# Dropping GpSimd's port waits from two feed-forward blocks and keeping them in the attention before them

## The chip, the cores and the metric

The program runs on one core of one Trainium2 chip. The metric is the time of one execution on the device, in microseconds. Four compute engines work at once and each takes its instructions in a fixed order: TensorE (PE; its weight loads are listed as PEld), VectorE (DVE), ScalarE (ACT) and GpSimd (POOL). SyncE (SP) issues the DMAs. Engines wait for one another through semaphores.

## What is computed

A causal attention with a decay (4 batches, 8 heads, 576 positions, head size 64), and behind it two feed-forward blocks on its output (2304 tokens, width 512, inner width 2048), all in float32:

```python
def _attn_ref(q, k, v, f):
    scores = scale * np.matmul(q, k.transpose(0, 1, 3, 2))
    cum = np.cumsum(np.log(np.clip(f, 0.0001, 1.0)), axis=-1)
    decay = cum[:, :, :, None] - cum[:, :, None, :]
    scores = np.where(causal, -1000000000.0, scores + decay)
    ...                                    # softmax over the last axis
    return np.matmul(attn, v)

def _moe_ref(x, w_in, w_out):              # first block
    h = x @ w_in
    g = np.where(h >= 1, h, np.where(h <= -1, 0.0, (h + 1) ** 2 / 4))
    return g @ w_out

def _moe2_ref(x, w_in, w_out, a, b):       # second block
    h = x @ w_in
    P = a[0] + a[1] * h + a[2] * h**2 + a[3] * h**3
    Q = 1.0 + np.abs(b[0]) * np.abs(h) + np.abs(b[1]) * h**2
    return (P / (Q + 1e-06)) @ w_out
```

## The kernel before

To reach float32's accuracy with TensorE's fp32r matmuls, every operand is split in a high and a low part: ScalarE writes the high part (a cast), and VectorE or GpSimd subtract it from the operand for the low one. Each product is then three matmuls: low by high, high by low, high by high. The tiles are named for this: `xh` and `xl` for the input of the first block, `gh` and `gl` for the activated values, `uh` and `ul` and parts of `arena` for the operands of the second block. The weights arrive as 64-bit floats, and VectorE converts them in four steps on tiles `wd` (each step 128 by 512 elements, SBUF to SBUF) behind one step of ScalarE.

The kernel runs in three stages. In the attention (to about 212 us in the trace), the matmuls of the first block's early part fill gaps. From about 212 to 540 us the first block runs in passes over chunks of 512 or 256 tokens; weights of the second block are converted and stored on the side (`t_q`, `wd`). From about 540 us the second block runs: its first product is made of seven smaller ones (L1059, a Winograd scheme of 2 by 2 blocks) on banks `h`, with additions on VectorE (`h<-h,us`), and its second product (L1085) adds into banks `a0` to `a3` (`b` in the trace).

The order of all instructions comes from a planner written out in the kernel. `plan` is a list scheduler: each task has ways (an engine with a duration), and the planner keeps a clock for each engine and picks the task that can start first. It has one more resource, `port`: VectorE tasks of the kind `dvp` (all inputs and the output in SBUF) and GpSimd's tasks share it, one at a time. For each GpSimd task that the plan starts less than `NEAR` = 1.0 us behind the end of the last `dvp` task, it notes that task in `behind` (L371 to L376). `emit` then issues the tasks in the planned order. Where a GpSimd task stands in `behind`, `emit` adds a dependency: the task's first GpSimd instruction waits for the last VectorE instruction of the noted task, though it needs no data of it. `Kept` (L18 to L31) is a wrapper that remembers what was issued on VectorE and GpSimd. The plan itself does not depend on whether that dependency is added.

`emit` is called twice, first for the attention (with `filling` set to `True`), then for the two blocks (`filling` is `False` there). The plan notes 93 GpSimd tasks in the first call and 72 in the second.

All VectorE and GpSimd instructions pass through the wrapper, so the trace shows them with one line, L26; they are told apart by their tiles.

Of the kernel before, what the change touches and what calls it, by code (L numbers as in the profile page):

```python
# [32 lines left out]
def kernel(ctx, tc, qT, kT, v, f, w_in1, w_out1, w_in2, w_out2, a, b, out):  # L33
    nc = tc.nc
    PE, ACT, DVE, POOL, SP = nc.tensor, nc.scalar, Kept(nc.vector), Kept(nc.gpsimd), nc.sync
# [267 lines left out]
    behind, given_to = {}, {}  # L303
# [837 lines left out]
    filling = True  # L1141
# [9 lines left out]
    for size, kind, x, k in pieces:  # L1151
        key = FS + (FE - FS) * sofar / whole
        sofar += size
        n = CH[x]
# [27 lines left out]
    for kk in range(KD):  # L1182
        n = CH[FILL]
# [24 lines left out]
    def emit(order):  # L1208

        for n, fn in order:  # L1210
            DVE.given, POOL.given = [], []
            fn()
            given_to[n] = DVE.given
            if n in behind and POOL.given and given_to[behind[n]]:
                tc.add_manual_dep(POOL.given[0].ins, given_to[behind[n]][-1].ins.name, after_it, reason="port")

    bufs.update({tag: [T0] * n for tag, n in N_BUF.items()})
    nudge(0)
    order_ = plan(0, WK)
    emit(order_)  # L1220
    filling = False
    att.close()
# [88 lines left out]
    for p, (m, x, fs) in enumerate(passes):  # L1311
        n = CH[x % NCH]
# [71 lines left out]
    n = QN  # L1384
# [117 lines left out]
    nudge(first)  # L1502
    order_ = plan(first, WKB)
    emit(order_)
    man.close()

# [45 lines left out]
```

## Time and profile before

| | |
|---|---|
| median of 3 runs | 947.63 us (947.58 to 947.81) |
| the profiled execution | 947.47 us, span 945.8 us |
| TensorE busy | 933.6 us (99% of the span) |
| VectorE busy | 738.6 us (78%) |
| ScalarE busy | 704.7 us (75%) |
| GpSimd busy | 443.2 us (47%) |

The span is the time from the first to the last instruction; the rest of the execution's time lies around it. An engine is busy while it executes an instruction of the program; waiting does not count, but an instruction that is held up after its start does, and appears longer. So the busy share alone doesn't tell a held engine from a working one; the duration of an instruction beside others of its shape does.

### The profile page before, as it was taken

The page shows a single profiled execution, that of the slowest core. Times are in us where ns is not written, and L with a number is a line of the kernel's source. Part 1 is how long each engine was busy: PE and PEld are TensorE (multiplying, and loading weights), DVE is VectorE, ACT ScalarE, POOL GpSimd, SP SyncE. Part 2 cuts the span into 40 slices and gives each one's busy share as a digit, 9 for nine tenths or more (in the row PEclk, how much of TensorE's full clock was granted, in tenths as well). Part 3 has the DMA queues.
Part 4 walks back from the last instruction along what each step waited for, and adds up shares of the span by engine and source line. Part 5 has one row for each costly group of instructions (what it writes and reads, how often), then busy time and mean ns, then how long its engine had stood idle before and what let it go on. Part 6 is the DMA issues. An engine that isn't in the chain of part 4 may idle for free.

```text
span 945.8 us, 16658 instructions
## 1 busy us (share of the span) xinstructions
PE 933.6 (99%) x5172; PEld 789.3 (83%) x5172; DVE 738.6 (78%) x1615; ACT 704.7 (75%) x1568; POOL 443.2 (47%) x542
## 2 busy tenths in 40 slices
PE   9899999999999999999999999999999999999998
PEld 6666877778888888888998888989898989898986
DVE  8989789873766987887557598899988888888840
ACT  7899888875765655655556599889988898878751
POOL 3655633636465222131222176666655556555553
PEclk9999999999999999999999999999999999999999
DMA  8788898846554477686947856877334473434100
GB/s 256 231 276 268 249 304 269 272 158 202 178 178 161 163 261 262 199 283 229 326 138 258 283 196 189 265 225 255 141 138 145 140 241 114 141 132 150 34 34 34
DMA packets 107489, 188.55 MB, mean 199 GB/s; under 512 B 13108, under 2 KB 43460, under 8 KB 107400
## 3 DMA queue, kind: packets, MB, share of 16 engines
q1 hardware_dynamic: 107400, 187.48, 59.9%
q8 instruction: 41, 0.67, 0.3%
q14 instruction: 48, 0.39, 0.1%
HBM read 142.72 MB, written 44.71 MB: 198 GB/s over the span
## 4 chain that ended last, share of the span: by engine, by line
PE 87%; DMA 5%; DVE 4%; ACT 2%; issue 1%; SPq 1%; POOL 0%; DVEq 0%; POOLq 0%; ACTq 0%
PE b L1085 21%; PE h L799 20%; PE h L1059 19%; PE a L901 18%; PE T L573 3%; PE O L610 2%; PE a L890 2%; DMA cb<-cd 2%; PE S L507 1%; DVE P L26 1%; DMA raw<-in_moe_w_in_dram 1%; PE S L498 1%; DVE wd L26 1%; DMA rcd<-rr 1%; ACT P L561 1%
## 5 line engine op out<-in xcount | busy, mean ns | idle before, releaser
L26 POOL TENSOR_TENSOR gl<-t,gh 128x512 fp32r<-128x512 f32 (+2 forms) x125 | 139.9, 1126 | 218.1 <-ACT gh L815 87.1
L1085 PE MATMUL b<-w,gh 128*128 128x512 f32 x576 | 179.1, 392 | 0.0
L901 PE MATMUL a<-gh,w 128*128 128x512 f32 (+1 forms) x576 | 161.8, 366 | 0.0
L26 POOL TENSOR_TENSOR t<-t,t 128x384 f32<-128x384 f32 x96 | 97.6, 1019 | 97.0 <-ACT t L847 77.9
L1085 PEld LDWEIGHTS b<-w,gh 128*128 128x128 f32 x576 | 108.0, 188 | 21.1
L26 DVE SCALAR_TENSOR_TENSOR t<-h,t 128x512 f32<-128x512 f32 (+2 forms) x125 | 73.7, 601 | 60.5 <-ACT t L831 59.7
L799 PE MATMUL h<-xh,arena 128*128 128x512 f32 (+1 forms) x400 | 120.1, 368 | 0.1
L901 PEld LDWEIGHTS a<-gh,w 128*128 128x128 f32 x576 | 104.0, 189 | 17.2
L1085 PE MATMUL b<-w,gl 128*128 128x512 f32 x288 | 112.0, 389 | 0.0
L815 ACT CAST gh<-t 128x512 fp32r<-128x512 f32 (+2 forms) x125 | 68.7, 553 | 49.4 <-PE a L901 25.5
L901 PE MATMUL a<-gl,w 128*128 128x512 f32 (+1 forms) x288 | 105.3, 366 | 0.0
L26 DVE SCALAR_TENSOR_TENSOR wd<-raw,wd 128x512 int32<-128x512 int32 x128 | 96.9, 758 | 2.6
L1059 PE MATMUL h<-arena,q 128*128 128x384 f32 x459 | 93.2, 336 | 0.0
L561 ACT ACTIVATE P<-P,nm 128x576 f32<-128x576 f32 (+2 forms) x144 | 83.7, 583 | 12.6 <-DVE nm L26 12.1
L826 ACT ACTIVATE t<-h 128x512 f32<-128x512 f32 (+1 forms) x77 | 42.5, 552 | 60.2 <-PE h L799 56.8
L26 DVE TENSOR_SCALAR wd<-wd 128x512 f32<-128x512 f32 (+1 forms) x128 | 67.1, 525 | 23.9 <-ACT wd L109 22.3
L1059 PEld LDWEIGHTS h<-arena,q 128*128 128x128 f32 x459 | 81.3, 188 | 4.5 <-DVE h L26 1.2
L799 PEld LDWEIGHTS h<-xh,arena 128*128 128x128 f32 x400 | 73.0, 188 | 12.9 <-DVE t L26 0.5
L799 PE MATMUL h<-xl,arena 128*128 128x512 f32 (+1 forms) x200 | 73.6, 368 | 0.0
L26 POOL TENSOR_SCALAR_AFFINE_SELECT cb<-cb 128x128 f32<-128x128 f32 (+1 forms) x150 | 43.8, 305 | 58.5 <-DVE wd L26 26.3
L26 DVE CUSTOM_DVE_ANT_0 P<-S,cb 128x256 f32<-128x256 f32 (+1 forms) x135 | 62.5, 477 | 10.6 <-POOL cb L26 4.3
L573 PE MATMUL T<-ident,P 128*128 128x128 f32 x400 | 63.5, 280 | 6.3 <-DVE PT L26 4.0
(171 smaller groups left out, 2214.5 us busy)
## 6 DMA issues: line engine op xcount, KB each, us to landing
q<-wqd SPq DMA_DIRECT2D x46, 512.0 KB, 3.7
raw<-in_moe_w_in_dram SPq DMA_DIRECT2D x32, 512.0 KB, 5.3
raw<-in_moe_w_out_dram SPq DMA_DIRECT2D x32, 512.0 KB, 4.1
arena<-wqd SPq DMA_DIRECT2D x26, 512.0 KB, 3.6
cb<-cd SPq DMA_DIRECT2D x15, 576.0 KB
xr<-xd SPq DMA_DIRECT2D x32, 256.0 KB, 3.3
wqd<-t SPq DMA_DIRECT2D x32, 256.0 KB, 3.8
wfd<-wd SPq DMA_DIRECT2D x26, 256.0 KB
```

What stands on the lines that cost most here:

```text
L26: self.given.append(getattr(self.engine, name)(*args, **kwargs))
L498: PE.matmul(t[:, 0:n1 - n0], lhs, rhs, start=(x == 0), stop=(x == len(ways) - 1))
L561: ACT.activation(p, p, AF.Exp, scale=-1.0, bias=nm[pr][:, pos:pos + 1], accum_out=ls[pr][:, COL[pos]:COL[pos] + 1])
L573: PE.transpose(ps[:, (c - c0) * P:(c - c0 + 1) * P], p[:, k0:k0 + P], ident[:])
L610: PE.matmul(o[pp, c_q:n], nat[pr, 2][:, c, pp], pt[:, c, j, c_q:n], start=(c == 0), stop=(c == ncs - 1),)
L799: PE.matmul(hps[g], ww[:, kk * P:(kk + 1) * P], xx[kk], start=(kk == 0 and y == 0), stop=(kk == KD - 1 and y == 2))
L815: ACT.copy(gt[g][0], mid[g][0][:, 0:n])
L826: ACT.activation(s[:, 0:n], hps[g], AF.Relu, scale=0.5, bias=0.5)
L890: PE.matmul(acc[x, d], ww[:, dd], gg, start=(part == 0 and g == gs[0]), stop=(part == 2 and g == gs[-1]))
L901: PE.matmul(acc[x, d], ww[:, dd], gg, start=(first and y == 0), stop=(last and y == 2))
L1059: PE.matmul(o, ww, xx, start=(new and i == 0 and z == 0), stop=(i == HQ - 1 and z == 2), skip_group_check=True,)
L1085: PE.matmul(acc[x, d], gg[:, dd], ww, start=(g == 0 and y == 0), stop=(g == NF - 1 and y == 2))
```

## The change

One condition more in `emit`: the dependency is added only while `filling` is true, which is the attention. In the two blocks a GpSimd instruction no longer waits for the VectorE operation noted in `behind`. The plan, the order of each engine's instructions and all other dependencies stay.

```diff
@@ -1211,7 +1211,7 @@
             DVE.given, POOL.given = [], []
             fn()
             given_to[n] = DVE.given
-            if n in behind and POOL.given and given_to[behind[n]]:
+            if filling and n in behind and POOL.given and given_to[behind[n]]:
                 tc.add_manual_dep(POOL.given[0].ins, given_to[behind[n]][-1].ins.name, after_it, reason="port")
```

## Rows read from the trace of the kernel before

**Rows 1.** Busy time by stretch: PE, PEld, DVE, ACT, POOL (instructions), clock, DMA.

```profile
540.00:640.00 100.00, 100.00 (x501) 89.56 (x500) 91.29 (x178) 88.17 (x184) 63.14 (x58) 1.00 0.68 219
```

**Rows 2.** Waits of PEld, 212 to 946 us: total us, times, longest; first and last.

```profile
PEld h L1059 <- DVE h L26: 1.2, 3, 0.4
...
PEld h L1059 <- DVE tailh L26: 0.3, 1, 0.3
```

**Rows 3.** Timeline at 229 us: start, us, engine, operation, [idle before <-releaser].

```profile
229.26 1.29 POOL L26 TENSOR_TENSOR arena<-wf,arena 128x512 fp32r<-128x512 f32 x1
229.35 1.75 DVE L26 TENSOR_TENSOR xl<-xr,xh 128x512 fp32r<-128x512 f32 x1 [0.34 <-ACT xh L783]
```

**Rows 4.** Timeline at 87 us, and the mask's group on the page (busy, mean ns).

```profile
86.83 1.36 DVE L26 SCALAR_TENSOR_TENSOR wd<-raw,wd 128x512 int32<-128x512 int32 x2
87.53 0.81 POOL L26 TENSOR_SCALAR_AFFINE_SELECT cb<-cb 128x128 f32<-128x128 f32 x1 [1.72 <-DVE wd L26]
88.11 0.84 DVE L26 TENSOR_TENSOR kl<-ks,kh 128x576 fp32r<-128x576 f32 x1
...
L26 POOL TENSOR_SCALAR_AFFINE_SELECT cb<-cb 128x128 f32<-128x128 f32 (+1 forms) x150 | 43.8, 305 | 58.5 <-DVE wd L26 26.3
```

**Rows 5.** Timeline 513 to 518 us, and the wd group on the page.

```profile
513.18 1.30 POOL L26 TENSOR_TENSOR gl<-t,gh 128x512 fp32r<-128x512 f32 x1 [3.82 <-DVE t L26]
513.78 1.45 DVE L26 TENSOR_SCALAR wd<-wd 128x512 f32<-128x512 f32 x2 [0.74 <-ACT wd L109]
514.65 0.61 ACT L815 CAST gh<-t 128x512 fp32r<-128x512 f32 x1
515.26 1.42 DVE L26 SCALAR_TENSOR_TENSOR wd<-raw,wd 128x512 int32<-128x512 int32 x2
516.85 1.30 POOL L26 TENSOR_TENSOR gl<-t,gh 128x512 fp32r<-128x512 f32 x1 [2.37 <-DVE wd L26]
517.33 0.19 PEld L799 LDWEIGHTS h<-xh,arena 128*128 128x128 f32 x1 [0.53 <-DVE t L26]
...
L26 DVE TENSOR_SCALAR wd<-wd 128x512 f32<-128x512 f32 (+1 forms) x128 | 67.1, 525 | 23.9 <-ACT wd L109 22.3
```

**Rows 6.** Timeline 541 to 549 us.

```profile
541.87 0.62 ACT L815 CAST gh<-t 128x512 fp32r<-128x512 f32 x1 [0.58 <-PE a L901]
...
544.64 0.56 DVE L26 COPY us<-h 128x384 f32<-128x384 f32 x1 [0.47 <-PE h L1059]
545.09 0.58 ACT L847 ACTIVATE t<-h,rt 128x384 f32<-128x384 f32 x1
...
545.58 1.02 DVE L26 TENSOR_TENSOR ul<-ul,uh 128x384 fp32r<-128x384 f32 x2
...
547.46 0.55 DVE L26 COPY us<-h 128x384 f32<-128x384 f32 x1
547.62 1.02 POOL L26 TENSOR_TENSOR t<-t,t 128x384 f32<-128x384 f32 x1 [2.58 <-DVE arena L26]
...
548.62 1.22 PE L1059 MATMUL h<-arena,q 128*128 128x384 f32 x6
```

**Rows 7.** Timeline 627 to 634 us.

```profile
627.55 0.58 ACT L847 ACTIVATE t<-h,rt 128x384 f32<-128x384 f32 x1
627.97 1.14 DVE L26 TENSOR_TENSOR xq<-xq,xq 128x384 f32<-128x384 f32 x2
...
629.25 1.01 POOL L26 TENSOR_TENSOR t<-t,t 128x384 f32<-128x384 f32 x1 [1.16 <-ACT tailh L850]
...
629.99 0.58 ACT L847 ACTIVATE t<-h,rt 128x384 f32<-128x384 f32 x1
630.02 0.67 DVE L26 TENSOR_TENSOR xq<-xq,xq 128x384 f32<-128x384 f32 x1
...
632.07 1.01 DVE L26 SCALAR_TENSOR_TENSOR t<-h,t 128x384 f32<-128x384 f32 x2
633.00 1.23 PE L1059 MATMUL h<-arena,q 128*128 128x384 f32 x6
```

## The prediction

> **What bounds the kernel now.** I read first the busy table by stretch, then TensorE's own waits, then GpSimd's, then the timeline around single waits. In the two blocks TensorE is the bound: from 540 to 640 us it is busy 100.00 of 100.00 us, beside VectorE at 91.29 and GpSimd at 63.14 [rows 1]. Its ends are modelled, so the better measure is what its weight loads wait for from 212 us on: four kinds of wait, the largest 1.2 us for VectorE's h, the smallest 0.3 us for VectorE's tailh, 2.3 us in all and none for GpSimd [rows 2]. So the most that this stretch can give back is about 2.3 us (0.24%), and no GpSimd wait is on that list. What can be lost has no such bound: TensorE takes its work in a fixed order, and each time that VectorE is later than a matmul's start, the delay goes to the end.
>
> **What the waits do.** The plan marks GpSimd operations that should start behind a VectorE operation which uses SBUF alone; in the blocks it marks 72 of them, in the attention 93. The 72 go, the 93 stay. No instruction, transfer or order on a queue is added, moved or removed; GpSimd's true waits (for ScalarE's data, for free buffers) stay. A GpSimd operation may therefore start as soon as its data and GpSimd itself are there.
>
> **The port, as the rows show it.** VectorE operations with both inputs in SBUF and GpSimd operations exclude one another, in both directions. GpSimd's split at 229.26 runs to 230.55; VectorE's xl, begun at 229.35, takes 1.75 us and ends 0.55 after GpSimd [rows 3]. The other way, GpSimd's mask at 87.53 takes 0.81 us where its group takes 0.305: it got the port about 0.14 us before VectorE's wd ended at 88.19. VectorE's next one, kl, began at 88.11, before wd had ended, and still came second: it ends at 88.95, 0.61 after GpSimd [rows 4]. So a GpSimd operation that becomes ready in the middle of a VectorE chain gets in at the next joint, and the rest of the chain is late by most of its 1.0 to 1.3 us. With the wait it goes behind the chain, where VectorE mostly has operations on PSUM that don't care: us at 547.46 takes 0.55 us although GpSimd runs from 547.62 [rows 6].
>
> The Trainium skill's page "SBUF — State Buffer", section "Who interferes with whom", says the same of the port: issue order decides who blocks, for the whole instruction. That speaks against this change, and the trace agrees (1.75 us for xl). The same page gives the loser's start as VectorE's end plus about 0.115 us (in its section on the wrong bandwidth-pool intuition). By that figure a chain whose next operation begins before the last has ended would keep the port, and the places below would cost nothing; the 88.11 row says otherwise, since kl began first and lost.
>
> **Where nothing changes.** If the awaited VectorE operation is already running when GpSimd is ready, the port holds GpSimd as the semaphore did. The gain is then 0.1 to 0.3 us of GpSimd time, which no TensorE wait asks for: 0. In the first block most chains are conversions of weights, needed several us later; the earlier GpSimd operation costs VectorE about 1 us there, hidden by VectorE's idle share (8.7 of 100 us even in the densest stretch [rows 1]; more before 540): 0, unless the chain ends in something that TensorE takes within 1 us. That is so in three places that I priced, in profile time.
>
> A, end of the first block, 513 to 517 [rows 5]. GpSimd's split at 513.18 had been idle 3.82 us, and would run in that idle time; the wd pair at 513.78 took 1.45 us, against 1.05 by its group's mean of 0.525, and would then end some 0.4 earlier. But the next split has its data at 515.26 (ScalarE's gh, 514.65 + 0.61). It gets in between the two wd of the pair that began at 515.26, now 0.4 earlier; the second ends about 0.55 after GpSimd (515.4 + 1.30 + 0.55 = 517.25 against 516.68). What follows there is the t that TensorE already waits 0.53 us for at 517.33. Cost 0.55; without the 0.4 in advance 0.95.
>
> B, start of the second block, 541 to 549 [rows 6]. VectorE splits the new operands just ahead of TensorE. Two GpSimd operations now get in: gl (its data stands at 541.87 + 0.62 = 542.49, in the middle of the chain), and t (data at 545.09 + 0.58 = 545.67 instead of 547.62). The first delays the chain by about 1.1, of which the 0.47 idle before us at 544.64 takes part, so 0.55 is passed on; the second lets VectorE's second ul of the pair at 545.58 go on only at about 547.1, which brings the lag to 1.4. The us that ends at 548.01 ends at 549.4; TensorE took it at 548.62, so with 0.06 us to start, 0.8 is lost. If the first is absorbed wholly, the lag is 0.83 and the loss 0.3. I take 0.8.
>
> C, 628 to 633 [rows 7]. The first t on GpSimd has its data at 628.13 (627.55 + 0.58) against a start at 629.25. It gets in between the two xq that begin at 627.97, and the second ends at 629.8 for 629.11: 0.7 late. The next t has data at 630.57, ready at about 630.65, and the next xq would now begin at 630.72 (630.02 + 0.7): whoever wins, VectorE is 0.7 or 1.4 late. The first of the two t at 632.07 ends at 632.61; TensorE starts on its bank at 633.00. Loss 0.35 or 1.05; I take 0.6, nearer the lower since 0.07 us decides.
>
> **Other early starts.** Of the rest, a few lie before work that TensorE takes within 1 us (splits of the next chunk's x, a copy of an output bank, a bank that VectorE frees). No row prices these as a whole. Bounds: 0, if all are hidden as in the first block, and 2.0, the price of B two and a half times. I take 0.5, nearer to 0 since most of the awaited operations are conversions. Below nothing is excluded for these, as TensorE waits for no GpSimd operation [rows 2], but B and C can be given back in part: at most the 2.3 us.
>
> **Sum.** 0.55 + 0.8 + 0.6 + 0.5 = 2.45 us on the profiled execution's 947.47 (span 945.8 and 1.67 around it): 949.92. The median of the runs stands 0.16 above that execution, so 950.1 us, +0.26%.
>
> **Rivals.**
> 1. The port does the waits' work: GpSimd is held at the port where it was held by the semaphore, or TensorE's lead is enough after all. Then only A, or less, is left: 947.6 to 949.4, no change that can be told. For it: the 2.3 us show that TensorE rides with little loss though VectorE is often stretched already (1.75 at 229.35 [rows 3]); against it: B and C, where the lead is 0.6 and 0.4.
> 2. Faster: GpSimd's results come up to 2 us earlier, ScalarE's logarithm behind t starts earlier, and the banks come free sooner. It decides where ScalarE waits for GpSimd, not for itself. At most the 2.3 us of [rows 2] would go: 945.3. Against it: those waits name VectorE, which gets later, not sooner. To be faster by over 1.9 us it would need nearly all.
> 3. Pile-up: VectorE has 8.7 us of idle in 100 [rows 1]; if each of some eight early starts there costs it 1.0, the idle is gone and VectorE is the bound from 540 to 640. Then A to C come in full (0.95 + 0.8 + 1.05) and the others at 2.0: +4.8, 952.4.
> 4. That the change does nothing at all is excluded: the marked waits are seen in the trace as GpSimd idle behind VectorE, 3.82 us before 513.18 [rows 5].
>
> **Chances.** A measurement here tells about 0.2% (1.9 us) from no change. Forecast (+1.9 to +3.6) 0.45; rival 1 0.42; rival 2 0.03; rival 3 0.10. So faster 0.03, same 0.42, slower 0.55. The range holds the forecast and nearly all of rival 1 and the lower end of rival 3: 947.5 to 952.2. The forecast's own range is 949.5 to 951.2.
>
> **What would show it.** GpSimd's idle time behind VectorE's wd, t and arena goes from the blocks. VectorE's busy time grows by 5 to 20 us, in stretched wd, arena, ul and xq groups, at unchanged counts. TensorE's waits for VectorE grow from 2.3 to about 5 us, at 517, 547 to 549 and 633. If VectorE's mean times don't grow, the port account is wrong; if they grow and TensorE's waits do not, the leads were longer than I read; if the total grows by over 5 us, a queue that I have not seen (the conversions feed stores and loads on SP) has become late.

## The result, and the profile after

| | before | after |
|---|---|---|
| median | 947.72 us (947.58 to 948.11) | 953.12 us (952.91 to 953.4) |
| span of the profiled execution | 945.8 us | 951.4 us |

The ratio is 1.0058, 95% interval [1.0045, 1.007]: 5.4 us slower. The sign was forecast; the size was not (950.1 us, at most 952.2).

The busy line of the page after:

```profile
PE 935.3 (98%) x5172; PEld 788.9 (83%) x5172; DVE 755.3 (79%) x1615; ACT 705.6 (74%) x1568; POOL 452.4 (48%) x542
```

The counts are those of before. VectorE is busy 16.7 us longer (738.6 before), GpSimd 9.2 (443.2 before): the same instructions, held after their start. Busy time by stretch, after, answers [rows 1]; the columns are those of that group:

```profile
540.00:640.00 100.00, 97.04 (x481) 85.85 (x481) 90.18 (x168) 84.46 (x175) 63.36 (x57) 1.00 0.66 215
```

TensorE, at 100.00 of 100.00 before, now loses 3 us between 540 and 640, at an unchanged clock. What its weight loads wait for from 212 us on, after, answers [rows 2] (total us, times, longest):

```profile
PEld h L1059 <- issue: 1.9, 1, 1.9
PEld h L1059 <- DVE h L26: 1.4, 4, 0.4
PEld h L1059 <- DVE t L26: 1.2, 1, 1.2
PEld h L1059 <- ACT arena L1026: 1.0, 1, 1.0
PEld b L1085 <- DVE osb L26: 0.9, 1, 0.9
PEld a L901 <- issue: 0.9, 1, 0.9
PEld a L901 <- DVE t L26: 0.4, 1, 0.4
PEld h L1059 <- ACT us L419: 0.3, 1, 0.3
```

That is 8.0 us for 2.3, 6.7 of it behind VectorE with the two "issue" rows, as these stand behind matmuls that themselves wait for VectorE (its t at 406.66, its h at 554.88).

The list gives waits, not where the time is lost for good. For that I paired TensorE's 5172 matmuls of two runs in order and took, for each, its start after minus its start before. The difference is a stair. Its steps, from the level ahead of a place to the level behind it, are the price of each place (they stand against the start of the matmul in the run before, in us):

| place | step after | priced at |
|---|---|---|
| 405.6, the matmuls of L901 (a), for VectorE's t | +0.71 | 0 ("hidden") |
| 467.9, L901 again | +0.50 | 0, or within the others' 0.5 |
| 517.3 (A) | -0.40 | +0.55 |
| 548.6 (B) | +0.85 | +0.8 |
| 551.1, the next sum of six | +1.78 | not seen |
| 633.0 (C) | +1.05 | +0.6 |
| 666.8, for an output bank | +0.74 | within the others' 0.5 |

Between the steps the stair is flat to 0.1 us, apart from a step back of 0.14 at 619 us and from the start-up: 0.5 us before 25 us here, and -0.1 to 1.0 in the runs below, whatever their edit. The seven steps sum to 5.2, the two medians differ by 5.4. A stair is made of one execution of each kernel; where several kernels below drop the same waits, their steps agree to 0.05 us, except at 468 and 517.

Three places in detail. The timeline after at 388 to 407 us, the place that had been called hidden (start, us, engine, operation; x2 is two in a row; the idle time before, and its releaser, in brackets):

```profile
388.31 1.42 POOL L26 TENSOR_TENSOR gl<-t,gh 128x512 fp32r<-128x512 f32 x1 [1.43 <-ACT gh L815]
388.62 2.39 DVE L26 SCALAR_TENSOR_TENSOR wd<-raw,wd 128x512 int32<-128x512 int32 x2
...
392.25 0.89 DVE L26 TENSOR_SCALAR wd<-wd 128x512 f32<-128x512 f32 x2 [0.65 <-ACT wd L109]
393.18 2.38 DVE L26 SCALAR_TENSOR_TENSOR wd<-raw,wd 128x512 int32<-128x512 int32 x2
393.39 1.62 POOL L26 TENSOR_TENSOR gl<-t,gh 128x512 fp32r<-128x512 f32 x1 [3.66 <-ACT gh L815]
...
401.12 1.85 POOL L26 TENSOR_TENSOR gl<-t,gh 128x512 fp32r<-128x512 f32 x1 [6.11 <-ACT gh L815]
401.13 0.69 DVE L26 SCALAR_TENSOR_TENSOR wd<-raw,wd 128x512 int32<-128x512 int32 x1
401.74 1.52 DVE L26 TENSOR_SCALAR wd<-wd 128x512 int32<-128x512 int32 x1
...
405.83 1.28 DVE L26 TENSOR_TENSOR t<-a,t 128x512 f32<-128x512 f32 x2
...
406.66 0.47 PE L901 MATMUL a<-gl,w 128*128 128x512 f32 x1 [0.46 <-DVE t L26]
```

A pair of wd takes 1.42 us when it runs alone; here 2.39, 2.38, and then a single wd 1.52 instead of 0.43. Three times about 1 us; the idle time before 392.25 takes up little of it, as ScalarE's wd that ends it comes later too. The t that began at 402.66 before begins at 405.83. TensorE had a lead of 2.23 us over it (403.34 to 405.57), which covers two of the three.

The timeline after at 543 to 555 us answers [rows 6]:

```profile
543.90 1.65 POOL L26 TENSOR_TENSOR gl<-t,gh 128x512 fp32r<-128x512 f32 x1 [1.14 <-ACT gh L815]
544.32 1.65 DVE L26 TENSOR_TENSOR arena<-arena 128x384 fp32r<-128x384 f32 x1
...
548.02 1.16 POOL L26 TENSOR_TENSOR t<-t,t 128x384 f32<-128x384 f32 x1 [2.47 <-ACT t L847]
548.37 1.69 DVE L26 TENSOR_TENSOR arena<-arena 128x384 fp32r<-128x384 f32 x2
...
549.98 0.55 DVE L26 COPY us<-h 128x384 f32<-128x384 f32 x1
...
550.67 1.28 PE L1059 MATMUL h<-arena,q 128*128 128x384 f32 x6 [0.63 <-ACT gh L815]
550.80 1.29 POOL L26 TENSOR_TENSOR gl<-t,gh 128x512 fp32r<-128x512 f32 x1 [1.62 <-ACT gh L815]
551.11 2.69 DVE L26 TENSOR_TENSOR arena<-arena 128x384 fp32r<-128x384 f32 x2
552.36 1.02 POOL L26 TENSOR_TENSOR t<-t,t 128x384 f32<-128x384 f32 x1 [0.27 <-ACT t L847]
...
554.19 0.55 DVE L26 TENSOR_TENSOR h<-h,us 128x384 f32<-128x384 f32 x1
...
554.88 1.28 PE L1059 MATMUL h<-arena,q 128*128 128x384 f32 x6 [1.54 <-DVE h L26]
```

GpSimd's idle time now ends with ScalarE's gh and t, not with VectorE's arena. Four GpSimd operations each hold an arena; the prediction followed the first two. The pair at 551.11 takes 2.69 us where two free ones take about 1.0: both are held, one by gl, one by the t behind it. The matmul at 550.67 is the one that stood at 548.62. Its wait is put down to ScalarE's gh, but VectorE's us, whose bank it takes, ends at 550.53, 0.14 us ahead of it, just as VectorE's h ends 0.14 ahead of the next sum (554.74 and 554.88).

C after, which answers [rows 7]:

```profile
630.10 1.02 POOL L26 TENSOR_TENSOR t<-t,t 128x384 f32<-128x384 f32 x1
630.14 1.40 DVE L26 TENSOR_TENSOR xq<-xq,xq 128x384 f32<-128x384 f32 x1
...
632.57 1.41 DVE L26 TENSOR_TENSOR xq<-xq,xq 128x384 f32<-128x384 f32 x2
...
637.70 0.79 PE L1059 MATMUL h<-arena,q 128*128 128x384 f32 x3 [0.79 <-DVE t L26]
```

The first xq is held whole (1.40 for 0.55), and TensorE waits for VectorE's t at the end.

### The profile page after: what moved, and what is told of

Its sections match the earlier page's. It is cut to its first block, busy times and chain, and to the rows that moved or that the text cites. A ratio compares the mean times of both kernels' runs of the same rounds, so it can differ in the third digit from the quotient of the medians.

```text
span 951.4 us, 16638 instructions
## 1 busy us (share of the span) xinstructions
PE 935.3 (98%) x5172; PEld 788.9 (83%) x5172; DVE 755.3 (79%) x1615; ACT 705.6 (74%) x1568; POOL 452.4 (48%) x542
## 4 chain that ended last, share of the span: by engine, by line
PE 85%; DVE 8%; DMA 3%; ACT 2%; issue 2%; POOL 0%; SPq 0%; DVEq 0%; ACTq 0%; POOLq 0%
PE b L1085 20%; PE h L799 19%; PE h L1059 18%; PE a L901 17%; PE T L573 3%; PE O L610 2%; PE S L507 2%; PE a L890 2%; DVE wd L26 2%; DVE P L26 2%; PE warm L692 1%; ACT P L561 1%; PE S L498 1%; DVE PT L26 1%; DVE t L26 1%
## 5 line engine op out<-in xcount | busy, mean ns | idle before, releaser
L26 POOL TENSOR_TENSOR gl<-t,gh 128x512 fp32r<-128x512 f32 (+2 forms) x125 | 146.3, 1177 | 212.9 <-ACT gh L815 168.0
L901 PE MATMUL a<-gh,w 128*128 128x512 f32 (+1 forms) x576 | 161.7, 366 | 0.0
L901 PEld LDWEIGHTS a<-gh,w 128*128 128x128 f32 x576 | 104.0, 189 | 17.1
L26 DVE SCALAR_TENSOR_TENSOR wd<-raw,wd 128x512 int32<-128x512 int32 x128 | 109.1, 854 | 2.6
L901 PE MATMUL a<-gl,w 128*128 128x512 f32 (+1 forms) x288 | 105.4, 366 | 0.7 <-DVE t L26 0.7
L26 DVE TENSOR_SCALAR wd<-wd 128x512 f32<-128x512 f32 (+1 forms) x128 | 64.7, 507 | 21.9 <-ACT wd L109 20.3
```

The costliest lines, as they stand in the source:

```text
L26: self.given.append(getattr(self.engine, name)(*args, **kwargs))
L901: PE.matmul(acc[x, d], ww[:, dd], gg, start=(first and y == 0), stop=(last and y == 2))
```

## Experiments: which waits carry the loss

All but one of them (the limit NEAR, below) edit the one condition in emit. The theory: of the 72 waits taken away, ten stand where a step begins, and only those ten matter; the port holds VectorE at the other places too, but TensorE's lead covers it. The rival: the loss is spread over the 72, as VectorE's grown busy time is.

**Ten waits put back into the changed kernel.**

```
-            if filling and n in behind and POOL.given and given_to[behind[n]]:
+            if n in behind and (filling or n in (2397, 2430, 2593, 2830, 3030, 2843, 3368, 3346, 3357, 3479)) and POOL.given and given_to[behind[n]]:
```

> The changed kernel, with ten of the 72 dropped waits put back: those of the GpSimd operations that got into VectorE's chains just ahead of the five places where TensorE fell behind (tasks 2397 and 2430 before 405 us, 2593 before 468, 2830, 3030 and 2843 at 541 to 551, 3368, 3346 and 3357 at 626 to 631, 3479 at 664). Theory (a few early starts in the wrong joints cost all of it): these ten bring the loss of about 5.2 us back, 947.7 to 948.7 us. What is left open between those ends is the place at 517 us, where no wait is put back: by the predicted price A it costs 0.55. Rival (the loss is spread over the 72, each early start costs VectorE and so TensorE a little): ten of 72 bring back a seventh of it, about 952.4 us.

Measured: 947.46 us, ratio to before 1.0001 [0.9992, 1.001].

```profile
PE 933.1 (99%) x5172; PEld 789.0 (83%) x5172; DVE 745.9 (79%) x1615; ACT 705.7 (75%) x1568; POOL 449.9 (48%) x542
```

VectorE still spends 7.3 us more than before, and nothing is lost. The 62 other waits are worth nothing that the time can tell (it tells about 1 us), and growth of VectorE's busy time is by itself no price. That the time lies under the expected range is due to 517 us: the stair steps back by 0.19 there, where the prediction had a cost of 0.55.

**The same ten dropped from the kernel before.**

```
-            if n in behind and POOL.given and given_to[behind[n]]:
+            if n in behind and n not in (2397, 2430, 2593, 2830, 3030, 2843, 3368, 3346, 3357, 3479) and POOL.given and given_to[behind[n]]:
```

> The kernel before, with only those ten waits dropped and the other 62 of the blocks kept. Theory (ten early starts cost all): 952 to 953.2 us, TensorE's steps at 405, 468, 548, 551, 633 and 667 us as in the changed kernel. Rival (spread over the 72): a seventh of the loss, about 948.5 us. Were both this and the kernel that keeps the ten in the middle, the loss would need both kinds together.

Measured: 953.25 us, 1.0061 [1.0048, 1.0075], the whole loss. The stair has steps at the same places: 0.74, 0.17, -0.40, 0.85, 1.77, 1.05, 0.77. The second, at 468, is 0.3 smaller than in the changed kernel: that part of it needs others of the 62 to be free as well. VectorE is busy 748.1 us: 9.5 us of holding cost 5.5, where the 7.3 of the run before cost 0.

**Every wait dropped, the attention's 93 as well.**

```
-            if n in behind and POOL.given and given_to[behind[n]]:
+            if n in behind and False and POOL.given and given_to[behind[n]]:
```

> All 165 marked waits dropped, those 93 of the attention too. If the joints of VectorE's chains are what the waits guard, the attention, where GpSimd's operations are mostly masks of 0.3 us and VectorE is busy 87 of 100 us, should lose less per wait than the blocks: 953 to 956 us. If a wait is worth the same everywhere (5.4 us for 72), the 93 cost 7 more: 960 us. If the attention's waits cost more than they guard, under 953.

Measured: 957.62 us, 1.0107 [1.0093, 1.0121], between the 953 to 956 and the 960 us of the expectation. So the 93 are worth about 4.5 us more. In the profiled execution (958.31 us) the stair has +1.3 at 44.6 us and some 2.6 more up to 58 us, then +0.97 at 167 us, of which 0.3 is back by 191. Busy time by stretch of this kernel, then of the kernel before:

```profile
46.00:48.00 2.00, 0.66 (x4) 0.47 (x5) 2.00 (x7) 0.85 (x3) 0.56 (x3) 0.86 0.83 269
48.00:50.00 2.00, 2.00 (x15) 1.88 (x16) 1.12 (x6) 2.00 (x6) 1.40 (x6) 0.50 0.97 370
```

```profile
48.00:50.00 2.00, 2.00 (x17) 1.32 (x16) 2.00 (x10) 2.00 (x8) 1.22 (x4) 1.00 1.00 388
```

TensorE is busy only 0.66 of the 2 us to 48, its longest wait there 1.23 us for VectorE's nm. Then the granted clock stands at 0.50 of full speed (1.2 GHz) from 48 to 50, where before it was 1.00. A matmul of 256 columns takes 0.52 us at 48.42, where two of 384 in a row took 0.34 at 43.58.

This fall is not the main part of what the 93 waits are worth. The last kernel below keeps all 93, and its profiled execution has the like: TensorE busy 0.87 of the 2 us from 38 to 40, and then (busy time by stretch)

```profile
42.00:44.00 2.00, 2.00 (x10) 0.99 (x9) 1.93 (x6) 1.17 (x3) 1.58 (x2) 0.50 0.75 280
```

And of the four executions with every wait dropped, the one with a mean granted clock of 1.0 took 956.94 us, 3.8 more than the changed kernel's median; the two at 0.996 took 958.31 and 958.87. So most of the 4.5 us comes without the fall. Where it comes from stays open, as the one trace of this kernel has the fall in it.

## Experiments: place A

**One wait dropped from the kernel before, that of the split at 513.18.**

```
-            if n in behind and POOL.given and given_to[behind[n]]:
+            if n in behind and n != 2778 and POOL.given and given_to[behind[n]]:
```

> The kernel before, with one wait dropped: that of the split that ran at 513.18 us after 3.82 us of idle (task 2778). Theory (a GpSimd operation that runs in an idle stretch of VectorE takes nothing, and frees the port for later): the wd at 513.78 is no longer stretched (0.98 to 0.43 us), VectorE is 0.5 earlier at the t that TensorE waited 0.4 to 0.5 for at 517.33, and that wait goes: 947.3 us, 0.3 to 0.4 less than before. Rival (an early start can only cost): 947.7 or more.

Measured: 947.35 us, 0.9999 [0.999, 1.0009]. The timeline of this kernel, against [rows 5]:

```profile
513.16 0.89 DVE L26 TENSOR_SCALAR wd<-wd 128x512 f32<-128x512 f32 x2 [0.73 <-ACT wd L109]
514.08 1.42 DVE L26 SCALAR_TENSOR_TENSOR wd<-raw,wd 128x512 int32<-128x512 int32 x2
```

The first pair is no longer held (0.89 for 1.45), and TensorE's wait at 517.33 is gone, a step of -0.40. It looks like a gain from the edit, and is not, though the time came out as the theory had it. In four kernels below that keep this wait and change something only after it, the same step is -0.40 too, and so it is with more waits (the next kernel). There the pair is held just as long, but begins 1 us earlier than in [rows 5], when ScalarE's wd is there:

```profile
512.77 1.46 DVE L26 TENSOR_SCALAR wd<-wd 128x512 f32<-128x512 f32 x2 [0.73 <-ACT wd L109]
```

In the nine profiled executions that lose nothing in the first block before this place, the pair begins at 511.96 to 513.78, whatever the waits. The profile on which A was priced has the latest start (513.78); one other has the same, and there TensorE was itself 1.9 us later. Of the nine, that profile alone has the wait of 0.53; one has 0.31 (the ten waits put back), and seven have none. The stall of 0.5 us was a draw of that execution.

**More waits: the limit for a mark from 1.0 to 2.0 us.**

```
-    NEAR = 1.0
+    NEAR = 2.0
```

> The kernel before with more waits, not fewer: the limit within which the plan marks a GpSimd operation to start behind a VectorE operation goes from 1.0 to 2.0 us. Theory (only about ten of the marked places stand ahead of something that TensorE takes soon, and they have their wait already): no change, 946.9 to 948.3, within 0.1% of before; GpSimd idle somewhat longer behind VectorE, TensorE's steps under 0.5 us in sum either way. Rival (a wait costs where it is not needed): slower by over 2 us.

Measured: 947.65 us, 1.0004 [0.9994, 1.0013], VectorE busy 739.5 us. Neither dearer nor cheaper, as it must be if the places that need a wait had one.

## Experiments: do the places add up, and how

**The first block's three of the ten, dropped.**

```
-            if n in behind and POOL.given and given_to[behind[n]]:
+            if n in behind and n not in (2397, 2430, 2593) and POOL.given and given_to[behind[n]]:
```

> The kernel before with three waits dropped, all in the first block: those of the gl operations of GpSimd that stood at 389.74, 402.22 and 463.25 us (the third early gl in the stretch before 405 us never had a wait of its own). Theory (the lags of VectorE add up over several conversions, and only their sum passes TensorE's lead of 2.23 us at 405.57 us): TensorE steps late by 0.6 to 0.8 us at 405.6 and by 0.2 to 0.5 at 468, gets 0.3 to 0.4 back at 517.3, and nothing changes from 540 us on: in all +0.4 to +1.2 us, 947.9 to 948.7, less than the timing tells from no change. Rival (in the changed kernel the delay at 405 us came from elsewhere, as from the start-up or from other dropped waits): no step at 405.6 or 468.

**And one of them alone.**

```
-            if n in behind and POOL.given and given_to[behind[n]]:
+            if n in behind and n not in (2397,) and POOL.given and given_to[behind[n]]:
```

> The kernel before with one wait dropped, that of the gl at 389.74 us. Theory (lags add up): this gl starts at about 388.3 and stretches one wd from 0.69 to about 1.66 us; VectorE's chain is then about 1 us late up to 402, under the lead of 2.23 us of its sum over TensorE, so that TensorE has no step at 405.6 us (under 0.1); time 947.3 to 947.8. Rival (each stretched conversion before that point is paid in full by TensorE): a step of about 0.97 us at 405.6.

Measured: with three, steps of +0.71 at 405.6, +0.18 at 468 and -0.40 at 517 (948.6 us, 1.0008 [0.9998, 1.0018]); with one, none at 405.6 (947.66 us, 0.9997 [0.9987, 1.0008]). The timeline of the second kernel:

```profile
388.42 1.42 POOL L26 TENSOR_TENSOR gl<-t,gh 128x512 fp32r<-128x512 f32 x1 [1.43 <-ACT gh L815]
388.72 2.39 DVE L26 SCALAR_TENSOR_TENSOR wd<-raw,wd 128x512 int32<-128x512 int32 x2
...
393.29 1.42 DVE L26 SCALAR_TENSOR_TENSOR wd<-raw,wd 128x512 int32<-128x512 int32 x2
```

One pair held as in the changed kernel (2.39), the next free (1.42): about 1 us of lag under a lead of 2.23, no loss. The loss is what the sum of the lags has above the lead, as the theory had it: three of about 1.0 less 2.23 is 0.8, for a step of 0.71. The two times alone could not tell it: both intervals hold 1.

**The two waits that B was priced on, dropped; then the one behind them alone.**

```
-            if n in behind and POOL.given and given_to[behind[n]]:
+            if n in behind and n not in (2830, 3030) and POOL.given and given_to[behind[n]]:
```

> The kernel before with two waits dropped, those of the gl at 543.74 and of the t at 547.62 us: the two that the prediction's place B priced at 0.8 us. Theory: TensorE steps late by 0.8 to 0.9 us at 548.6 and by no more than 0.3 at 551.1, since the gl at 549.78 keeps its wait: +0.8 to +1.2 us in all, 948.3 to 948.7. Rival (the 1.67 us that the changed kernel lost at 551 us is what the first two carry on): 0.85 at 548.6 and 1.2 to 1.7 at 551.1, +2.0 to +2.5 in all.

```
-            if n in behind and POOL.given and given_to[behind[n]]:
+            if n in behind and n not in (2843,) and POOL.given and given_to[behind[n]]:
```

> The kernel before with one wait dropped, that of the gl at 549.78 us. Its data and GpSimd stand at 548.64, 0.05 us after VectorE's arena has begun (548.59). Theory: the gl gets in at the joint before the next arena (549.06), which then ends at about 550.4 instead of 549.61; the h that TensorE takes at 551.07 ends 0.8 later, at about 551.35, and TensorE steps late by 0.3 to 0.5 us at 551.1, by nothing at 548.6. Rival (this one gl and the unmarked t behind it carry all of the 1.67 us seen at 551 in the changed kernel): 1.2 to 1.7 at 551.1. Second rival (the port passes to VectorE's next operation, which began first): no step.

Measured: the two give +0.85 at 548.6 and +0.11 at 551 (948.72 us, 1.0008 [0.9999, 1.0018]); the one gives +0.80 at 551.1 and nothing at 548.6 (948.36 us, 1.0006 [0.9996, 1.0016]), more than the 0.3 to 0.5 worked out. In the changed kernel the three together lost 0.85 + 1.78: 0.87 more than apart. The timeline of the second kernel shows why, against that of the changed one:

```profile
548.24 2.11 DVE L26 TENSOR_TENSOR arena<-arena 128x384 fp32r<-128x384 f32 x2
548.24 1.70 POOL L26 TENSOR_TENSOR gl<-t,gh 128x512 fp32r<-128x512 f32 x1
549.90 1.32 POOL L26 TENSOR_TENSOR t<-t,t 128x384 f32<-128x384 f32 x1
550.28 0.54 DVE L26 TENSOR_TENSOR tailh<-h,tailh 128x384 f32<-128x384 f32 x1
550.74 0.55 DVE L26 TENSOR_TENSOR h<-h,us 128x384 f32<-128x384 f32 x1
```

Here the first arena of the pair keeps the port and gl waits 0.4 us for it (1.70 for 1.30); only the second arena is held, and until later than worked out, as gl itself was late. The t that follows (549.90) meets tailh and h, which read a bank of PSUM and take their 0.55. In the changed kernel VectorE is later against GpSimd, gl holds the first arena, and the t meets the second one (551.11, 2.69 for the pair).

**C and the output bank: their four waits dropped; then the first of C's two alone.**

```
-            if n in behind and POOL.given and given_to[behind[n]]:
+            if n in behind and n not in (3368, 3346, 3357, 3479) and POOL.given and given_to[behind[n]]:
```

> The kernel before with four waits dropped, all after 620 us: those of the t operations of GpSimd that stood at 627.08, 629.25 and 630.83 us (the prediction's place C) and at 665.63 us (a split ahead of VectorE's copy of an output bank, priced only within the others' 0.5). Theory (the prices of places that lie apart add up, and each is what it was in the changed kernel): TensorE steps late by 0.9 to 1.1 us at 633.0 and by 0.6 to 0.8 at 666.8, +1.5 to +1.9 us in all, 949.1 to 949.6. Rival (they cost that much only on top of the lag that the earlier places leave): under 1.0 us together.

```
-            if n in behind and POOL.given and given_to[behind[n]]:
+            if n in behind and n not in (3346,) and POOL.given and given_to[behind[n]]:
```

> The kernel before with one wait dropped, that of the t at 629.25 us, the first of the two early starts from which the prediction made its place C. Prediction's working: this t gets in between the two xq of the pair, one of them is about 0.7 us late, 0.35 us reach TensorE at 633.0, and the t at 630.83, which keeps its wait, adds nothing: a step of 0.35, at most 0.5. Rival (the full 1.05 comes from one early start, since the two that follow move with it): 0.9 to 1.1 at 633.0. Second rival (it takes all three): no step above 0.1.

Measured: the four give +1.05 at 633.0 and +0.74 at 666.8 (949.43 us, 1.0018 [1.0008, 1.0028]), as in the changed kernel: these places lie far apart, and their prices add. The one gives +0.35 at 633.0, the prediction's lower end. Its time (947.66 us, 1.0005 [0.9994, 1.0015]) can't tell so little; the profiled execution (949.3 us) also lost 1.3 us in the attention around 40 us, where no wait was changed and the granted clock fell (shown above).

```profile
628.56 2.32 POOL L26 TENSOR_TENSOR t<-t,t 128x384 f32<-128x384 f32 x2 [0.69 <-DVE xq L26]
...
629.45 1.84 DVE L26 TENSOR_TENSOR xq<-xq,xq 128x384 f32<-128x384 f32 x2
...
632.89 1.01 POOL L26 TENSOR_TENSOR t<-t,t 128x384 f32<-128x384 f32 x1 [2.01 <-DVE xq L26]
```

The freed t is the second of the two at 628.56; it holds one xq of the pair, 1.84 for 1.1, 0.7 late as priced. The next t still stands behind its xq (632.89). With all four freed the loss of 1.05 is put together otherwise (timeline of that kernel):

```profile
626.01 1.01 POOL L26 TENSOR_TENSOR t<-t,t 128x384 f32<-128x384 f32 x1
626.06 1.39 DVE L26 TENSOR_TENSOR xq<-xq,xq 128x384 f32<-128x384 f32 x1
...
630.79 0.84 DVE L26 TENSOR_TENSOR xq<-xq,xq 128x384 f32<-128x384 f32 x1
```

The t whose wait ended at 627.08 before, which the prediction did not count, holds the first xq whole (1.39 for 0.55). The two that it did count then stand 0.6 us ahead of their xq and hold them by 0.3 each. This is read from the timeline; no run freed that t alone.

## Why the prediction was right and wrong, point by point

**The steps that failed, in one sum.** The forecast added 0.55 (A), 0.8 (B), 0.6 (C), 0.5 for all other places and 0 for the first block: 2.45 us. The stair has -0.40, 0.85, 1.05 and, in place of the 0.5 and the 0, 3.7. So what failed in the main is not the port but the list of places where VectorE's lag reaches TensorE.

**The bound and the mechanism held.** TensorE is the bound, VectorE's holding at the port is the price, and the waits of TensorE that grow name VectorE. VectorE's busy time grew by 16.7 us, in the forecast 5 to 20. Of the wd groups the one in [rows 5] did not grow (64.7 us), and another did (SCALAR_TENSOR_TENSOR, from 96.9 to 109.1 us). The idle time of GpSimd's gl behind wd from 212 us on went from 60.3 us in 15 waits to one of 4.9; behind arena it is gone. Rival 1 fell (six places lost 0.5 to 1.8 us each). Of rival 2 there is a trace: at 619 us TensorE's wait of 0.27 us for VectorE's tailh [rows 2] is gone, and the stair steps back by 0.14, in the three kernels in which the 62 waits are gone, and in no other. A's -0.40 is not the change's. The Trainium skill's page "SBUF — State Buffer", section "Who interferes with whom", has it that issue order decides who blocks; the timelines here agree, but for starts within 0.01 us of each other (last section).

**A, +0.55, was wrong in sign.** The split does hold the second wd pair as priced, 2.53 us instead of 1.42 (timeline after):

```profile
515.18 2.53 DVE L26 SCALAR_TENSOR_TENSOR wd<-raw,wd 128x512 int32<-128x512 int32 x2
```

But the term started from a stall of 0.53 us that the kernel doesn't always have. The step that failed is taking one execution's stall as the kernel's own. In the kernel with the ten waits put back, which frees this split too, the pair is held as long (2.53) and TensorE waits 0.31 us here, less than in the profile before; against the -0.40 of the executions without a stall, its -0.19 leaves 0.2 us for the split, not 0.55.

**B, +0.8, was right:** 0.85, in the changed kernel and with its two waits alone. The working stopped too soon, though. It didn't follow VectorE's order on to the next sum of six, 2.5 us later, where a third freed gl and the unmarked t behind it took 1.78.

**C, 0.35 or 1.05: the sizes came out, the working of the larger one did not.** The first of its two t alone costs 0.35, as priced. The 1.05 of the changed kernel does not come from the second one's race for 0.07 us: a third t ahead of them, left out of the count, costs most of it. That it equals the larger case is chance. Taking 0.6 between two cases was not a case at all.

**The first block, 0, was the wrong step.** The criterion was "unless the chain ends in something that TensorE takes within 1 us", which prices each early start by itself. Lags of about 1 us add up along VectorE's chain until some idle time takes them up, and in 388 to 403 us there is little. Three of them against a lead of 2.23 lost 0.7; one alone lost nothing. The right test was the sum of the lags since VectorE's last idle time, against the lead of the next result that TensorE takes. The third early gl had no mark, and came early because the ones before it did: counting marks alone misses such followers, here as at 552.36.

**Others, 0.5, bounds 0 to 2.0, mis-sized.** What was not in A, B and C comes to 0.71 + 0.50 + 1.78 + 0.74 = 3.7 us, the first block's 0 included. The upper bound was two and a half times B, for want of a row. The rows to find the places were there: before, TensorE's lead over the VectorE result in question is 2.23 us at 405.6 and under 0.7 at the other five. So those five meet the prediction's own test ("within 1 us"), and only B's and C's were looked up; how many places without a loss a list of such leads would hold too was not counted. Hence also the upper end of 952.2. Rival 3, 952.4 with VectorE as the bound, came near to the time, by luck: from 540 to 640 us VectorE is busy 90.18 us of 100, so it is not the bound.

**"Over 5 us: a queue I have not seen"** was a wrong reading in advance. The total grew by 5.4, ten waits carry all of it, and none of TensorE's waits from 212 us on names a DMA.

## What to carry to other kernels

A wait that only arranges who goes first is worth what it saves the bound engine at the next result which that engine takes: sum the lags from the helper's last idle time, and set the sum against the lead. Follow the helper's order past the first loss, with the operations that move along unmarked. Before pricing a stall of half a microsecond in one profile, see whether the kernel has it in another execution; here one of the three priced places was a draw. The same holds for a fall of the granted clock.

## What the runs showed of the hardware that was not expected

The loser need not have two inputs in SBUF, as the prediction had it: TENSOR_SCALAR of wd, with one, is held the same way, 1.52 us for 0.43 at 401.74 after, and 1.46 for a pair of 0.89 at 512.77 with more waits. [rows 5] has it before the change, 1.45 for the pair. The Trainium skill's page "SBUF — State Buffer", section "Who interferes with whom", lists tensor_scalar among those that can take the shared pair in a two-port mode; the rows agree as to the holding, and do not show the mode.

Who wins a joint between two operations turns on 0.2 us here. After, gl (401.12) and wd (401.13) both begin while the wd of 400.80 runs: wd passes unheld in 0.69, gl takes 1.85 for 1.30, and the next wd pays. At 548.24, in the kernel with one wait dropped, gl and arena begin together, and arena passes too. With the first block's three waits dropped, the same gl begins 0.22 ahead of the wd, and goes first:

```profile
401.00 1.46 POOL L26 TENSOR_TENSOR gl<-t,gh 128x512 fp32r<-128x512 f32 x1 [5.89 <-ACT gh L815]
401.22 1.78 DVE L26 SCALAR_TENSOR_TENSOR wd<-raw,wd 128x512 int32<-128x512 int32 x1
```

Either way one VectorE operation is held for 1.1 us: the race moves the loss to another instruction and not away.

The granted clock fell in the attention, in two of the profiled executions: after TensorE had been busy 0.66 of 2 us in the one (every wait dropped) and 0.87 of 2 us in the other (one late wait dropped), it stood at 0.50. So such a fall also comes with all 93 waits of the attention kept, and what it costs in one trace can't be put down to dropping them.
